# Attention followed by an FFN with x − tanh x: the clamps of the output weights' words go from VectorE to GpSimd, half of the first scalings to ScalarE, and the first batch is planned anew

## The chip, the cores and the metric

The kernel runs on one core of a Trainium2 chip. The time is in device microseconds, from the start to the end of one execution; the kernel before takes 1252.24 us (median of 3 runs, 1252.01 to 1252.95). Engines are named as in the profile: PE is TensorE's matmul, PEld its weight load, DVE is VectorE, ACT is ScalarE, POOL is GpSimd, SP issues DMAs.

## The reference

Keys and values are one tensor: `kv` pooled over windows of 4 by 4 and multiplied by `w_sr`. The output of the attention is the input of the FFN, whose activation is h − tanh h.

```python
B, C, H, W, N = 4, 128, 384, 32, 384 * 32
kv_pool = kv.reshape(B, H // 4, 4, W // 4, 4, C).mean(axis=(2, 4))
k = v = kv_pool.reshape(B, -1, C) @ w_sr           # 768 keys
s = (q @ k.transpose(0, 2, 1)) / np.sqrt(C)
a = np.exp(s - s.max(-1, keepdims=True))
x = (a / (a.sum(-1, keepdims=True) + 1e-9)) @ v    # 4 * 12288 tokens of 128
h = x @ w_in                                       # 128 -> 2048
return (h - np.tanh(h)) @ w_out                    # 2048 -> 128
```

`w_in` and `w_out` reach the kernel as 64-bit floats, so each weight is two 32-bit words that the kernel has to turn into one 32-bit float.

## The kernel before

The four batches are cut into 96 groups of 512 tokens, 24 to a batch. Tokens lie along the free axis, channels along the partitions. For each group `attention` makes scores in three pieces of 1024 columns (`scores`, PE, L1071), a root of them on ACT (`roots`, L1075, tile `p`), its square on POOL (`beyond`, L1078, tile `r2`, printed `r` in the profile), and the sum with the values on PE (`values`, L1121). Beside it goes a linear part: `upper_linear` (PE, L1093), `linear` (ACT, L1096, `yk`), `along` (POOL, L1099, `m`), `shares` (PE, L1102), `share_left` (ACT, L1105, `t`), `fewer` (DVE, L1111, `dy`), then `apart` (DVE, L1125, `dl`) and `rounded` (POOL, L1128, `dr`). The tiles of `y`, `den` and `num` share one bank of PSUM, `x`, one after the other. `feed_forward` multiplies `dr` by `winr` in eight pieces (`forth`, PE, L1178), squares them on ACT (L1182, `u`), makes cubes of them on DVE (L1185, `r`), and sums them with `Wr` and some smaller terms in one bank, `acc` (PE, L1197, L1164, L1168); `result` (DVE, L1208) takes it out.

Ahead of a batch's first group stands its preparation. For the first batch:

- `words_of` turns the words of a quarter of `w_in` or of `w_out` into floats: `size` (ACT, L438, the absolute value), `within` (DVE, L441, a clamp from above and below), `shift` (DVE, L444), `upper` (DVE, L448), `lower` (ACT, L454), `add` (DVE, L457). There are four quarters of each matrix. Every tile of 128x512 that `within` and `shift` use is one half of a tile of the ring `r` (for `w_out`).
- `keys` pools the keys (DVE, L588, and by halving sums on POOL, L582), takes their mean (`mean`, `centre`, L631) and multiplies by `w_sr` (L640, L652, L657).
- `about_centre` expands the FFN about the centre. `first` (PE, L764) gives the centre's h in the PSUM tile `prep` (bank `acc`). `first_chain`, 18 small DVE instructions on tiles of 128x16 (L850 to L876), gives slopes and their inverse, `third_order_apart` (seven more, L882 to L888) the third order. `by_first` (DVE, L953) scales a quarter of `winT` by g1, which lies in `prep`, into the tile `Wg`; `beside` (ACT, L961) puts a column of 4 from `prep` next to it; `slopes` (PE, L965) multiplies `Wg` by a quarter of `w_out` into `prep`. `spread` (PE, L936) and `scaled` (DVE, L943) scale `w_in` by the inverse into `winr`; `by_third` (POOL, L978) scales `w_out` by the third order into `Wr`. `turn_slopes`, `upper_slopes`, `joined_slopes`, `upper_joined` and `lower_joined` (L997 to L1011) end it.

Nothing runs in the order of the source. Each piece of work is handed to `Plan.op` with a step, an engine, an assumed duration (`us`), what it reads and writes, and its code. `Plan.run` starts what is ready in order of step, on assumed durations, and emits the code in the order in which it started it; each engine then runs its instructions in that order. `MOVES` is a table of numbers that are added to the steps. Where the planner treats two parts of one tile as apart, the waits between engines are still set by the framework for the emitted order. Names below carry the number of the buffer (`Wg_397`) where rows would read alike.

Of the kernel before, what the change touches and what calls it, by code (L numbers as in the profile page):

```python
# [207 lines left out]
def attention_then_ffn(ctx: ExitStack, tc: tile.TileContext, q, kv_by_key, kv_by_place, w_sr, w_in,  # L208
# [187 lines left out]
    def words_of(step, load_step, n, kind):  # L396
# [31 lines left out]
        def y(dt=F32):  # L428
            return plan[ym][:, 0].bitcast(dt)
# [1070 lines left out]
```

## Time and profile before

| | |
|---|---|
| median of 3 runs | 1252.24 us (1252.01 to 1252.95) |
| the profiled execution | 1249.61 us |
| its span, first to last instruction | 1247.9 us |
| PE busy | 1208.5 us (97%) |
| DVE busy | 1147.2 us (92%) |
| ACT busy | 1142.6 us (92%) |
| POOL busy | 1055.6 us (85%) |

The profile comes from one execution of 1249.61 us, of which 1.7 us lie outside the span. Times in its rows are counted from the start of the span. Busy time of PE is modelled from pipelined instructions, so the number of matmuls in a stretch says more than its share.

### The profile page before, as it was taken

Reading aid. Unit: us, or ns where it says so; the run is one execution under the profiler, and the core shown is the slowest. Engines: PE = TensorE matmul, PEld = TensorE weight load, DVE = VectorE, ACT = ScalarE, POOL = GpSimd, SP = SyncE. Lnnn points to the kernel's source line nnn. Section 1 sums busy time; section 2 is a strip of 40 time slices with the busy share of each in tenths; the row PEclk is TensorE's granted clock in tenths of the full one; section 3 lists DMA queues with packets and bytes.
Section 4 is the critical chain, followed back from the end, with each engine's and each line's share of the span. In section 5 each row is a group of like instructions: output and inputs, shape, how many; then the busy total and the mean of one; then the engine's idle time right before and its main releaser. Section 6 shows DMA issues by size and latency. Waiting matters only on the chain.

```text
span 1247.9 us, 16674 instructions
## 1 busy us (share of the span) xinstructions
PE 1208.5 (97%) x5252; PEld 929.5 (74%) x5252; DVE 1147.2 (92%) x1218; ACT 1142.6 (92%) x1373; POOL 1055.6 (85%) x836
## 2 busy tenths in 40 slices
PE   5899999999999999999999999999999999999997
PEld 4677777777777777777777777777777777777774
DVE  6789999989999999998999999999899999999997
ACT  3689998999999999999999998999999999999995
POOL 4599988799998887889999887789988888888881
PEclk8999999999999999999999999999999999999999
DMA  9134511125541111111563111111111111111101
GB/s 362 53 85 101 113 50 43 35 85 110 118 93 43 50 45 43 41 54 60 120 124 87 47 47 43 43 43 58 54 44 45 49 43 43 43 45 50 35 26 35
DMA packets 41713, 84.49 MB, mean 68 GB/s; under 512 B 5040, under 2 KB 7216, under 8 KB 41616
## 3 DMA queue, kind: packets, MB, share of 16 engines
q1 hardware_dynamic: 35904, 66.82, 16.1%
q0 software_dynamic: 5712, 16.52, 7.9%
q8 instruction: 44, 0.72, 0.2%
q14 instruction: 53, 0.43, 0.1%
HBM read 57.93 MB, written 25.39 MB: 67 GB/s over the span
## 4 chain that ended last, share of the span: by engine, by line
PE 80%; POOL 7%; DVE 5%; ACT 3%; issue 2%; DMA 2%; SPq 0%; DVEq 0%; ACTq 0%
PE big L1178 26%; PE acc L1197 24%; PE big L1071 9%; PE x L1121 9%; PE acc L1164 5%; POOL r L1078 3%; DVE r L1185 2%; PE x L1093 2%; PE x L1102 2%; PE acc L1168 1%; ACT u L1182 1%; ACT p L1075 1%; DMA winr<-in_kv_by_key_dram 1%; POOL dr L1128 1%; PE x L965 1%
## 5 line engine op out<-in xcount | busy, mean ns | idle before, releaser
L1185 DVE SCALAR_TENSOR_TENSOR r<-big,u 128x1024 fp32r<-128x1024 f32 x768 | 901.7, 1219 | 76.6 <-ACT u L1182 64.3
L1182 ACT ACTIVATE u<-big 128x1024 f32<-128x1024 f32 x768 | 762.4, 1028 | 42.1 <-PE big L1178 38.9
L1078 POOL TENSOR_TENSOR r<-p 128x1024 fp32r<-128x1024 f32 x288 | 562.9, 1961 | 107.9 <-ACT p L1075 107.5
L1178 PE MATMUL big<-dr,winr 128*128 128x512 f32 x1536 | 487.2, 407 | 5.0 <-ACT p L1075 2.7
L1197 PE MATMUL acc<-r,Wr 128*128 128x512 f32 x1536 | 451.3, 394 | 2.4 <-DVE o L1208 1.8
L1178 PEld LDWEIGHTS big<-dr,winr 128*128 128x128 f32 x1536 | 269.7, 188 | 107.9 <-DVE r L1185 29.7
L1197 PEld LDWEIGHTS acc<-r,Wr 128*128 128x128 f32 x1536 | 286.6, 188 | 68.9 <-DVE o L1208 2.6
L1075 ACT ACTIVATE p<-big 128x1024 f32<-128x1024 f32 x288 | 296.6, 1030 | 14.7 <-POOL r L1078 3.2
L1071 PE MATMUL big<-qr,kTr 128*128 128x512 f32 x576 | 185.7, 404 | 1.7 <-ACT p L1075 1.7
L1121 PE MATMUL x<-r,vvr 128*128 128x512 f32 x576 | 165.7, 396 | 1.2 <-POOL r L1078 0.8
L1128 POOL TENSOR_TENSOR dr<-dl,yk 128x512 fp32r<-128x512 f32 x96 | 130.4, 1358 | 40.4 <-DVE dl L1125 40.0
L1071 PEld LDWEIGHTS big<-qr,kTr 128*128 128x128 f32 x576 | 100.9, 188 | 40.9 <-ACT p L1075 22.5
L1115 POOL TENSOR_TENSOR ql<-q,qr 128x512 fp32r<-128x512 f32 x96 | 131.1, 1366 | 0.2
L1099 POOL TENSOR_TENSOR m<-yk,q 128x512 fp32r<-128x512 f32 x96 | 130.7, 1361 | 0.0
L1121 PEld LDWEIGHTS x<-r,vvr 128*128 128x128 f32 x576 | 108.5, 189 | 26.9 <-POOL r L1078 1.5
L1208 DVE TENSOR_SCALAR o<-acc,At 128x512 f32<-128x512 f32 x96 | 71.3, 743 | 1.5 <-PE acc L1168 1.5
L1111 DVE SCALAR_TENSOR_TENSOR dy<-x,yk 128x512 f32<-128x512 f32 x96 | 65.4, 681 | 1.6 <-ACT t L1105 1.6
L1056 POOL TENSOR_SCALAR qr<-q 128x512 fp32r<-128x512 f32 x96 | 65.8, 686 | 0.9 <-DMA q<-in_q_dram 0.7
L1125 DVE TENSOR_TENSOR dl<-x,dy 128x512 fp32r<-128x512 f32 x96 | 65.4, 681 | 0.3
L1096 ACT ACTIVATE yk<-x 128x512 f32<-128x512 f32 x96 | 57.9, 604 | 7.5 <-PE x L1093 6.4
L1164 PE MATMUL acc<-qr,Lh 128*128 128x512 f32 x192 | 60.4, 396 | 0.0
L1105 ACT ACTIVATE t<-x 128x512 f32<-128x512 f32 x96 | 57.8, 602 | 2.7 <-PE x L1102 2.3
(195 smaller groups left out, 629.7 us busy)
## 6 DMA issues: line engine op xcount, KB each, us to landing
q<-in_q_dram SPq DMA_DIRECT2D x96, 256.0 KB
out_dram<-o SPq DMA_DIRECT2D x96, 256.0 KB
kvp<-in_kv_by_place_dram POOLq DMA_DIRECT2D x21, 768.0 KB, 7.4
kc<-inverse SPq DMA_DIRECT2D x12, 256.0 KB
kvp<-in_kv_by_place_dram SPq DMA_DIRECT2D x3, 768.0 KB
winr<-in_kv_by_key_dram SPq DMA_DIRECT2D x4, 512.0 KB
r<-in_kv_by_key_dram SPq DMA_DIRECT2D x4, 512.0 KB
Wr<-in_kv_by_key_dram SPq DMA_DIRECT2D x4, 512.0 KB
```

What stands on the lines that cost most here:

```text
L1071: PE.matmul(out=half(plan[s], h), lhsT=plan[kTr][:, n * P : (n + 1) * P], rhs=plan[qr], start=True, stop=True)
L1075: A.activation(out=plan[p], in_=plan[s], func=AF.Silu, scale=1.0 / 3)
L1078: PL.tensor_tensor(out=plan[r], in0=plan[p], in1=plan[p], op=ALU.mult)
L1099: PL.tensor_tensor(out=plan[m], in0=plan[yk], in1=plan[qs], op=ALU.mult)
L1115: PL.tensor_tensor(out=plan[ql], in0=plan[qs], in1=plan[qr].bitcast(F32), op=ALU.subtract)
L1121: PE.matmul(out=plan[num], lhsT=plan[vvr][:, n], rhs=half(plan[f"r2.{g}.{k}"], h), start=(start and h == 0), stop=(stop and h == 1))
L1128: PL.tensor_tensor(out=plan[dr], in0=plan[dl].bitcast(F32), in1=plan[yk], op=ALU.add)
L1164: PE.matmul(out=plan[acc], lhsT=x, rhs=plan[y], start=(start and n == 0), stop=(stop and n == 2))
L1178: PE.matmul(out=half(plan[hp], h), lhsT=plan[winr][:, f * P : (f + 1) * P], rhs=plan[dr], start=True, stop=True)
L1182: A.activation(out=plan[u], in_=plan[hp], func=AF.Square)
L1185: V.scalar_tensor_tensor(out=plan[r], in0=plan[hp], scalar=1.0, in1=plan[u], op0=ALU.add, op1=ALU.mult)
L1197: PE.matmul(out=plan[acc], lhsT=plan[Wr][:, 2 * n + h], rhs=half(plan[r], h), start=(start and h == 0), stop=(stop and h == 1))
```

## The change

Four things are changed. `within` of `w_out`'s words runs on POOL, with an assumed duration of 0.66 us, and has a step of its own. `first_chain` gets one more DVE instruction, which copies g1 from `prep` to SBUF (`x(4)`). In the first batch the second and the fourth quarter (`n` odd) of `winT` are scaled by `pair_by_first` on ACT, two times two instructions of 128x128 for each, in place of one `by_first` on DVE. And the entries of `MOVES` for the first batch and for the first three groups are new; those of the other batches stand as they were.

```diff
     MOVES = {
-        "load.i.0": -4159.973, "words.i.0": -2510.035, "load.i.1": -4127.904, "words.i.1":
+        "load.i.0": -7340.706, "words.i.0": -3260.585, "load.i.1": -7340.702, "words.i.1":
...
         def within():
-            V.tensor_scalar(out=y(), in0=m(), scalar1=TOP, scalar2=BOTTOM, op0=ALU.min, op1=ALU.max)
+            E = V if kind == "i" else PL
+            E.tensor_scalar(out=y(), in0=m(), scalar1=TOP, scalar2=BOTTOM, op0=ALU.min, op1=ALU.max)
...
-        plan.op(step, "DVE", 0.36, within, (M,), (Y,), port=True)
+        plan.op(at(step, "within", kind, n), *(("DVE", 0.36) if kind == "i" else ("POOL", 0.66)), within, (M,), (Y,),
+                port=True)
...
             V.tensor_reduce(out=stat[:, b : b + 1], in_=z, op=ALU.add, axis=AX.X)
+            line(x(4), g1, 1.0, 0.0)
...
-            plan.op(known, on, 3.4, first_chain, ((prep, "h"),), ((prep, "t"), (hb, 8), iv, ("stat", b)))
+            plan.op(known, on, 3.55, first_chain, ((prep, "h"),), ((prep, "t"), (hb, 8), (hb, 4), iv, ("stat", b)))
...
-            if b:
+            if b or n % 2:
                 for k in range(2):
-                    plan.op(at(slopes_at[n], "pair", c, n, k), "ACT", 0.6, partial(pair_by_first, k), (gg, "winT"),
+                    plan.op(at(slopes_at[n], "pair", c, n, k), "ACT", 0.6, partial(pair_by_first, k),
+                            (gg if b else (hb, 4), "winT"),
                             ((wg, 2 + k),), late=0.1)
```

The lines of the kernel after are 3 to 7 higher than before (L1078 becomes L1085, L441 becomes L445).

On POOL, where the first batch's preparation gives way to the first groups (`q` to `qr` and `ql`, then the squares `r2`), there stood before:

```order
L1056 TENSOR_SCALAR qr_244<-q_193 128x512
L1056 TENSOR_SCALAR qr_251<-q_196 128x512
L1115 TENSOR_TENSOR ql_264<-q_196,qr_251 128x512
L1078 TENSOR_TENSOR r2_372<-p_340 128x1024
L1099 TENSOR_TENSOR m_383<-yk_351,q_141 128x512
```

and stands now:

```order
L1063 TENSOR_SCALAR qr_246<-q_193 128x512
L1063 TENSOR_SCALAR qr_253<-q_198 128x512
L1122 TENSOR_TENSOR ql_264<-q_198,qr_253 128x512
L445 TENSOR_SCALAR r_271<-r_271 128x512
L445 TENSOR_SCALAR r_279<-r_279 128x512
L445 TENSOR_SCALAR r_313<-r_313 128x512
L445 TENSOR_SCALAR r_320<-r_320 128x512
L1085 TENSOR_TENSOR r2_367<-p_333 128x1024
L1085 TENSOR_TENSOR r2_378<-p_372 128x1024
L1106 TENSOR_TENSOR m_400<-yk_376,q_123 128x512
```

The four clamps stand between the last `ql` and the first square, and `m` of the first group comes behind two squares where it came behind one.

On ACT, at the end of `first_chain` (`Wg` is the scaled quarter, `acc` the tile `prep`), with the semaphores that a row waits for, there stood before:

```order
L961 COPY Wg_392<-acc_259 128x4 [waits DVE_49]
L961 COPY Wg_397<-acc_259 128x4 [waits DVE_49]
L1105 ACTIVATE t_406<-x_399 128x512 [waits PE_49]
L961 COPY Wg_409<-acc_259 128x4 [waits DVE_49]
L1075 ACTIVATE p_425<-big_389 128x1024 [waits Pool_49]
```

and stands now:

```order
L967 COPY Wg_389<-acc_266 128x4 [waits DVE_49]
L964 ACTIVATE Wg_397<-winT_68,hb_347 128x128 x4
L967 COPY Wg_397<-acc_266 128x4 [waits DVE_49,PE_49]
L967 COPY Wg_418<-acc_266 128x4
L1082 ACTIVATE p_422<-big_386 128x1024 [waits Pool_49]
L1112 ACTIVATE t_431<-x_424 128x512 [waits PE_49]
```

The first group's `t` has moved behind a root (`p_422`), and the second column copy now waits for PE too.

On DVE, from the first group's `dy` to its `dl`, there stood before:

```order
L1111 SCALAR_TENSOR_TENSOR dy_431<-x_399,yk_351 128x512
L943 TENSOR_TENSOR winr_433<-big_401,win32_67 128x1024
L953 TENSOR_TENSOR Wg_409<-winT_68,acc_259 128x4x128
L953 TENSOR_TENSOR Wg_445<-winT_68,acc_259 128x4x128
L1125 TENSOR_TENSOR dl_457<-x_437,dy_431 128x512
```

and stands now:

```order
L1118 SCALAR_TENSOR_TENSOR dy_433<-x_424,yk_376 128x512
L949 TENSOR_TENSOR winr_441<-big_392,win32_67 128x1024
L949 TENSOR_TENSOR winr_441<-big_459,win32_67 128x1024
L452 SCALAR_TENSOR_TENSOR wout32_69<-Wr_203,r_320 128x512
L461 ISA wout32_69<-wout32_69,o_316 128x1024
L1132 TENSOR_TENSOR dl_481<-x_443,dy_433 128x512
```

The second half of `winr` and two steps of `w_out`'s words (the last quarter's `upper`, the third quarter's `add`) have come ahead of `dl`; the two scalings L953 between them are gone.

## Rows read from the trace of the kernel before

**Rows 1.** The page: the span.

```profile
span 1247.9 us, 16674 instructions
```

**Rows 2.** Busy time by stretch: start:end, length, PE and other engines with counts.

```profile
60.00:80.00 20.00, 18.79 (x75) 13.28 (x75) 14.52 (x15) 17.18 (x22) 18.64 (x14) 1.00 0.21 46
80.00:100.00 20.00, 19.25 (x78) 13.74 (x79) 17.45 (x17) 18.71 (x22) 19.26 (x15) 1.00 0.46 100
...
100.00:1200.00 1100.00, 1092.68 (x4699) 839.68 (x4698) 1031.81 (x1056) 1045.97 (x1249) 968.55 (x753) 1.00 0.23 61
```

**Rows 3.** Timeline of POOL: start, duration, instruction, count, idle time before and its releaser.

```profile
28.67 1.31 POOL L1056 TENSOR_SCALAR qr<-q 128x512 fp32r<-128x512 f32 x2 [0.71 <-DMA q<-in_q_dram]
30.07 1.33 POOL L1115 TENSOR_TENSOR ql<-q,qr 128x512 fp32r<-128x512 f32 x1
37.83 2.08 POOL L1078 TENSOR_TENSOR r<-p 128x1024 fp32r<-128x1024 f32 x1 [6.43 <-ACT p L1075]
...
51.25 1.27 POOL L1128 TENSOR_TENSOR dr<-dl,yk 128x512 fp32r<-128x512 f32 x1 [3.33 <-DVE dl L1125]
```

**Rows 4.** Timeline of ACT.

```profile
28.94 0.66 ACT L438 ACTIVATE r<-winr 128x512 f32<-128x512 f32 x1
...
42.39 0.60 ACT L1105 ACTIVATE t<-x 128x512 f32<-128x512 f32 x1
...
44.88 1.02 ACT L1075 ACTIVATE p<-big 128x1024 f32<-128x1024 f32 x1 [0.54 <-POOL r L1078]
```

**Rows 5.** Timeline of DVE, from the words of w_out to the first chain.

```profile
29.63 0.63 DVE L441 TENSOR_SCALAR r<-r 128x512 f32<-128x512 f32 x1 [1.27 <-ACT r L438]
30.30 1.39 DVE L444 TENSOR_SCALAR r<-r 128x512 int32<-128x512 int32 x1
...
37.02 0.42 DVE L444 TENSOR_SCALAR r<-r 128x512 int32<-128x512 int32 x1
...
38.08 0.17 DVE L853 TENSOR_SCALAR hb<-acc 128x16 f32<-128x16 f32 x1
```

**Rows 6.** Timeline of DVE, behind the first chain.

```profile
42.53 0.69 DVE L953 TENSOR_TENSOR Wg<-winT,acc 128x512 f32<-128x512 f32 x1 [0.23 <-ACT Wg L961]
...
47.76 1.23 DVE L943 TENSOR_TENSOR winr<-big,win 128x1024 fp32r<-128x1024 f32 x1 [2.26 <-PE big L936]
...
50.49 0.68 DVE L1125 TENSOR_TENSOR dl<-x,dy 128x512 fp32r<-128x512 f32 x1
...
54.51 1.56 DVE L457 CUSTOM_DVE_ANT_0 wout<-wout,o 128x1024 uint16<-128x1024 uint16 x1
```

**Rows 7.** Timeline of PE, from the first slopes to the first forth.

```profile
45.05 1.13 PE L965 MATMUL acc<-Wg,wout 128*128 128x129 f32 x8 [2.43 <-DVE hb L888]
...
47.38 2.67 PE L1121 MATMUL x<-r,vvr 128*128 128x512 f32 x6
...
51.59 0.47 PE L1102 MATMUL x<-m,share 128*128 128x512 f32 x1
...
53.91 1.56 PE L1178 MATMUL big<-dr,winr 128*128 128x512 f32 x6
```

**Rows 8.** PE by stretch of one microsecond: busy, granted clock, DMA.

```profile
45.00:46.00 1.00, 0.95 (x8) 1.00 0.00 0
46.00:47.00 1.00, 1.00 (x8) 0.62 0.00 0
...
48.00:49.00 1.00, 1.00 (x4) 0.50 0.00 0
```

**Rows 9.** Timeline of POOL, from the first wait behind the preparation on.

```profile
60.08 1.90 POOL L1078 TENSOR_TENSOR r<-p 128x1024 fp32r<-128x1024 f32 x1 [2.88 <-ACT p L1075]
...
65.53 1.90 POOL L1078 TENSOR_TENSOR r<-p 128x1024 fp32r<-128x1024 f32 x1 [1.28 <-ACT p L1075]
...
75.43 1.36 POOL L541 DMA_DIRECT2D kvp<-in_kv_by_place_dram  x1
...
93.06 1.29 POOL L1128 TENSOR_TENSOR dr<-dl,yk 128x512 fp32r<-128x512 f32 x1 [0.61 <-DVE dl L1125]
```

161 rows, old and new, of the table MOVES are left out of this document.

## The prediction

> **What bounds the kernel now.** I first read the busy time by stretch [rows 2]. From 100 to 1200 us PE is busy for 1092.68 of 1100 us with 4699 matmuls, 0.234 us each: in that part PE sets the time. From 60 to 80 us it does 75 matmuls and from 80 to 100 us 78, where 20 us at 0.234 would hold 85.4; some 18 are missing, 4.2 us of PE. Everything that this change touches lies ahead of 100 us. From about the 290th instruction on, the order on PE is the same before and after, so the change is worth what it shifts the point at which the common part begins. I take as that point the end of the fourth group's `dr` on POOL, 93.06 + 1.29 = 94.35 us [rows 9]; with it PE begins the fourth group's `forth`, and from there PE is nearly dense.
>
> Back from that point the chain is read engine by engine. POOL waits until 60.08 us for a root, once more 1.28 us at 65.53 and 0.61 us at 93.06 [rows 9], and hardly between. The root at 60.08 hangs on the first group's `forth` at 53.91 [rows 7], this on `dr` (51.25, after 3.33 us of waiting) and `dl` (50.49), `dl` on the first `values` (47.38), and these on the first `slopes` (45.05), which waited 2.43 us for the end of the third order on DVE [rows 3, 6, 7]. The third order follows `first_chain`, which begins at 38.08, when DVE is through with the words of `w_out`, begun at 29.63 [rows 5]. That is the path: words, first chain, slopes, values, `dl`, `forth`, root, POOL.
>
> **The clamps.** Four L441 leave DVE for POOL. On POOL the nearest row is the same kind of instruction on the same shape, two L1056 in 1.31 us, so 0.655 us each and 2.6 us for four; POOL idles 6.43 us ahead of 37.83 [rows 3], so they cost POOL nothing. But the order puts them behind the last `ql`, which ends at 30.07 + 1.33 = 31.40 [rows 3]; the first result is there at 32.05, where DVE had begun at 29.63. Ahead of it on PE, three more key products come before `centre` and delay the input from ACT (L438, 28.94 + 0.66 = 29.60 [rows 4]) by 3 x 0.234 = 0.7 us to 30.3; this is hidden behind `ql`, and would cost as much if `ql` were gone.
>
> From 29.63 to 38.08 DVE ran 15 instructions, 0.563 us each on average. The order leaves nine ahead of `first_chain`: besides the four clamps, one `upper` and one `add` have been put off. At the same average they take 5.1 us, so `first_chain` would start at 37.1. That is one bound. The other comes from L444 at 30.30: it took 1.39 us where the one at 37.02 took 0.42, and ended with POOL's `ql`, which was running [rows 3, 5]. DVE's steps here all stand beside clamps on POOL, and each may be held until a clamp ends; two such holds of 0.655 make it 38.4. I take the middle, 37.8: a gain of 0.3 where the removed instructions alone promise 1.0.
>
> The Trainium skill, "SBUF — State Buffer", section "Who interferes with whom", says that GpSimd and a VectorE instruction in its two-port mode, or with two SBUF inputs, exclude each other for a whole instruction, whichever starts first. The row of L444 agrees. By that rule alone every step of the words can be held, the first chain would start at the later bound, and the sum would come out 0.6 us above mine.
>
> **The first scalings.** From the start of `first_chain` to the first `slopes` it was 45.05 - 38.08 = 6.97 us [rows 5, 7]. One `by_first` that stood in between goes to ACT, 0.69 us and its wait of 0.23 [rows 6]; the copy of g1 adds about 0.2 (a small step takes 0.17 [rows 5]). So 6.25 us, and `slopes` starts at 37.8 + 6.2 = 44.0, 1.0 earlier.
>
> Here a new wait comes in. The second `beside` on ACT now also waits for PE: it reads `prep`, and the first `slopes` that writes `prep` has been emitted ahead of it. It can run only when that is done, 44.0 + 1.13 = 45.2 [rows 7]. Queued behind it on ACT are a root and then the first group's `t`. Before, `t` ran at 42.39, ahead of both [rows 4]. Now it ends at 45.2 + 1.02 + 0.60 = 46.8 [rows 4]. `dy` on DVE waits for `t` (0.69, priced like L953, of the same size [rows 6]) until 47.5, and the first group's `values` wait for `dy`, since `num` takes the bank of `den`. So `values` start at 47.5, against 47.38: the gain of 1.0 is used up. The four scalings on ACT themselves lie in this wait and cost nothing; without it they would hold ACT for two instructions' time each.
>
> **From `values` to `forth`.** Before, the six `values` stood together and `dl` came at 50.49 [rows 6]. Now four `values`, four `slopes` and eight `spread` come first: 16 x 0.234 = 3.7 us, to 51.2. DVE has to wait for these, because the second half of `winr` (1.23 [rows 6]) stands ahead of `dl` in its queue: 52.5. Then come the `upper` and the `add` that were put off, 2 x 0.563: 53.6. Then `dl`, 0.68: 54.3, where before it ended at 51.17. The third `slopes` and the third `by_third` wait for that `add` as well; on PE it ends at 53.6 + 1.13 = 54.7. From the second group's `shares`, next on PE, to `forth` it was 53.91 - 51.59 = 2.32 [rows 7]. So `forth` starts at 57.0, 3.1 us later. If an `add` beside POOL takes 1.56 like the one at 54.51 [rows 6], it is up to 0.9 more.
>
> **What comes back.** With `forth` 3.1 later, the root for which POOL waited until 60.08 comes at 63.2 too. From there to the fourth `dr` POOL ran 34.27 us, of which it waited 1.28 + 0.61 = 1.9 [rows 9]; with POOL later than the roots that it needs, these waits go. The squares, `dr`, `qr`, `ql` and `m` in that stretch are as many as before; one more DMA issue of the keys stands in it (1.36 [rows 9]), and `lower_joined` has gone out of it: I take 0.5 for both, from 0 to 1.4. The lag at the fourth `dr` is then 3.1 - 1.9 + 0.5 = 1.7 us, and PE carries it to the end.
>
> **Sum.** The profiled execution took 1249.61 us, 1247.9 of them the span [rows 1]. With 1.7 more it would take 1251.3. The median of the runs is 2.6 above the profiled one; I carry that over unchanged: 1252.24 + 1.7 = 1253.9 us. About 0.2%, 2.5 us, is what a measurement of this kernel can tell from no change; 1.7 lies inside.
>
> **Rivals.**
> (a) Slower: PE's clock falls while it waits. Before, it was granted 1.00 until 46 us, then 0.62 in one microsecond and 0.50, the lower level of 1.2 GHz, at 48 [rows 8], after PE had waited 2.43 us for `slopes`; the six `values` took 2.67 us, six `forth` 1.56 at the upper level [rows 7], 0.185 more each, and some ten products lay in it: 1.9 us. I have assumed that PE keeps 2.4 GHz through its new wait for `dy`, from 44.0 + 9 x 0.234 = 46.1 to 47.5. If it doesn't, the 16 products before the second half of `winr` pay the 1.9, all of it on the path: lag 3.6, 1255.8 us. Against it speaks that `slopes` start 1.0 earlier and PE's gaps are shorter; for it, that two gaps stand where one stood. It decides from 0.8 us on. Chance 0.31, with what else adds up to as much.
> The Trainium skill, "TensorE: Matmul & The Clock Gate", section "What's actually happening", says that the lower clock is the default and activity lifts it; the fall after the wait in these rows agrees.
> (b) Faster: the front isn't late. If `t` isn't held behind `slopes` and the root (1.13 + 1.02) and the first chain starts at 37.1 (0.7), `forth` starts at 57.0 - 2.9 = 54.1, the lag is -1.2 at the fourth `dr`, and if POOL's new order closes half of the 4.2 us of missing matmuls, -3.3: 1248.9 us. For it: DVE loses six long instructions ahead of `forth`; against it, the wait of the column copy that stands in the order. Chance 0.17.
> (c) The clamps relieve nothing: held at every step, the chain starts at 38.4, and all follows as above: 1254.5 us. That is inside the forecast's case, which with all that stays within 0.2% has 0.52.
>
> **Numbers.** Forecast 1253.9 us. The range goes down to 1250.0, a lag of -2.2, most of the way to (b), and up to 1256.5, (a) with 0.7 of the held `add`. Faster by over 0.2% 0.17, within 0.2% 0.52, slower by over 0.2% 0.31.
>
> **What would show it.** In the profile after, `first_chain` (L858) should begin near 37.8; a clamp on POOL should take 0.6 to 0.7 us; the second L967 should wait for PE until 45; L1112 should start near 46 and `values` (L1128) near 47.5; `dl` (L1132) near 53.6, `forth` (L1185) near 57.0; the fourth L1135 should end near 96. PE's granted clock should stay at 1.00 from 43 to 52. I am wrong if `t` comes ahead of the root's 1 us, if `dl` doesn't wait for the second half of `winr`, or if PE runs denser than before from 60 to 100 us.

## The result: 0.55% slower

The changed kernel takes 1258.09 us (median of 4 runs, 1257.37 to 1260.39) against 1252.12 for the kernel before (4 runs, 1251.23 to 1252.95): a ratio of 1.0055, with a 95% interval of 1.0043 to 1.0067, so 6.0 us by the medians (6.9 by the ratio, 5.4 to 8.4) where 1.7 were forecast, and above the range. The two profiled executions took 1257.83 and 1249.61 us and lie 8.2 apart. So places are read from the traces here, and sizes from the ratios.

The page and the busy time by stretch of the changed kernel, as in [rows 1, 2]:

```profile
span 1256.1 us, 16687 instructions
```

```profile
60.00:80.00 20.00, 17.15 (x72) 12.31 (x72) 13.86 (x14) 15.38 (x21) 13.96 (x11) 0.98 0.26 50
80.00:100.00 20.00, 19.54 (x80) 13.82 (x79) 16.58 (x17) 18.76 (x22) 19.27 (x14) 1.00 0.63 135
100.00:1200.00 1100.00, 1091.62 (x4691) 838.20 (x4690) 1030.51 (x1055) 1045.00 (x1247) 966.74 (x754) 1.00 0.22 60
```

Behind 100 us PE does 4691 matmuls where it did 4699, 8 fewer of 0.234 us, so little of the loss stands there. From 60 to 80 us POOL is busy for 13.96 us instead of 18.64: most of the loss stands ahead of 80 us.

The first weights landed 0.53 us later in this trace: ScalarE's first step on them started at 5.37 us instead of 4.84. Nothing is taken off the times below for it. e2, which has the same order, started at 4.88 and still reaches `first_chain` at 38.77, where the changed kernel has 38.72.

POOL, the timeline, as in [rows 3, 9]:

```profile
31.96 1.19 POOL L445 TENSOR_SCALAR r<-r 128x512 f32<-128x512 f32 x2
34.79 0.78 POOL L445 TENSOR_SCALAR r<-r 128x512 f32<-128x512 f32 x1 [1.64 <-ACT r L441]
...
55.66 1.26 POOL L1135 TENSOR_TENSOR dr<-dl,yk 128x512 fp32r<-128x512 f32 x1
...
65.71 3.75 POOL L1085 TENSOR_TENSOR r<-p 128x1024 fp32r<-128x1024 f32 x2 [0.47 <-ACT p L1082]
...
71.49 1.88 POOL L1085 TENSOR_TENSOR r<-p 128x1024 fp32r<-128x1024 f32 x1 [0.69 <-ACT p L1082]
...
99.05 1.31 POOL L1135 TENSOR_TENSOR dr<-dl,yk 128x512 fp32r<-128x512 f32 x1
```

DVE, the timeline, as in [rows 5, 6]:

```profile
32.61 0.82 DVE L448 TENSOR_SCALAR r<-r 128x512 int32<-128x512 int32 x1 [2.94 <-POOL r L445]
...
35.01 1.10 DVE L452 SCALAR_TENSOR_TENSOR wout<-winr,r 128x512 int32<-128x512 int32 x1
...
38.72 0.17 DVE L858 TENSOR_SCALAR hb<-acc 128x16 f32<-128x16 f32 x1
...
52.15 1.23 DVE L949 TENSOR_TENSOR winr<-big,win 128x1024 fp32r<-128x1024 f32 x1 [2.84 <-PE big L942]
53.30 0.68 DVE L452 SCALAR_TENSOR_TENSOR wout<-Wr,r 128x512 int32<-128x512 int32 x1
53.89 0.69 DVE L461 CUSTOM_DVE_ANT_0 wout<-wout,o 128x1024 uint16<-128x1024 uint16 x1
54.50 0.69 DVE L1132 TENSOR_TENSOR dl<-x,dy 128x512 fp32r<-128x512 f32 x1
...
77.79 0.74 DVE L1215 TENSOR_SCALAR o<-acc,At 128x512 f32<-128x512 f32 x1
```

ACT, the timeline, as in [rows 4]:

```profile
45.81 0.23 ACT L967 COPY Wg<-acc 128x4 f32<-128x4 f32 x2 [2.35 <-PE acc L971]
45.92 1.04 ACT L1082 ACTIVATE p<-big 128x1024 f32<-128x1024 f32 x1
46.84 0.62 ACT L1112 ACTIVATE t<-x 128x512 f32<-128x512 f32 x1
...
64.62 1.02 ACT L1082 ACTIVATE p<-big 128x1024 f32<-128x1024 f32 x1
```

PE, the timeline, as in [rows 7], and PE's granted clock (the figure behind the bracket) by the microsecond, as in [rows 8]:

```profile
44.65 1.13 PE L971 MATMUL acc<-Wg,wout 128*128 128x129 f32 x8 [1.38 <-DVE hb L894]
...
48.24 1.20 PE L1128 MATMUL x<-r,vvr 128*128 128x512 f32 x4 [1.33 <-DVE dy L1118]
...
54.64 1.16 PE L971 MATMUL acc<-Wg,wout 128*128 128x129 f32 x8 [2.05 <-DVE wout L461]
...
57.49 0.79 PE L1100 MATMUL x<-qr,Mh 128*128 128x512 f32 x1 [1.46 <-DVE dy L1118]
58.08 1.05 PE L1185 MATMUL big<-dr,winr 128*128 128x512 f32 x2
58.94 1.88 PE L971 MATMUL acc<-Wg,wout 128*128 128x129 f32 x8
```

```profile
57.00:58.00 1.00, 0.51 (x1) 0.61 0.02 10
58.00:59.00 1.00, 1.00 (x4) 0.50 0.07 16
59.00:60.00 1.00, 1.00 (x6) 0.50 0.00 0
60.00:61.00 1.00, 1.00 (x6) 0.68 0.00 0
```

The forecast wait is there: the column copy L967 waits 2.35 us for PE's `slopes`, a root stands behind it, then `t`. What was not forecast stands further on. Behind two waits of PE, 2.05 us for the words and 1.46 us for the second group's `dy`, the clock falls to its lower level, 1.2 GHz, and the fourth `slopes` take 1.88 us instead of 1.13. The root for which POOL waits comes at 64.62, 5.6 us later than before, and the first result (L1215) 6.0 later, though the first `forth` is only 4.2 later. The same two places in the kernel before:

```profile
58.98 1.02 ACT L1075 ACTIVATE p<-big 128x1024 f32<-128x1024 f32 x1
```

```profile
71.78 0.74 DVE L1208 TENSOR_SCALAR o<-acc,At 128x512 f32<-128x512 f32 x1
```

### The profile page after: what moved, and what is told of

Same layout as the page of the kernel before. It is cut to its first block, busy times and chain, and to the rows that moved or that the text cites. A ratio compares the mean times of both kernels' runs of the same rounds, so it can differ in the third digit from the quotient of the medians.

```text
span 1256.1 us, 16687 instructions
## 1 busy us (share of the span) xinstructions
PE 1210.9 (96%) x5252; PEld 930.7 (74%) x5252; DVE 1143.7 (91%) x1213; ACT 1145.1 (91%) x1381; POOL 1057.3 (84%) x840
## 4 chain that ended last, share of the span: by engine, by line
PE 85%; DVE 5%; ACT 4%; issue 2%; DMA 2%; POOL 1%; SPq 0%; ACTq 0%; DVEq 0%; POOLq 0%
PE big L1185 27%; PE acc L1204 25%; PE big L1078 10%; PE x L1128 9%; PE acc L1171 5%; DVE r L1192 3%; ACT u L1189 2%; PE x L1100 2%; PE x L1109 2%; PE acc L1175 2%; ACT p L1082 1%; PE x L971 1%; DMA Wr<-in_kv_by_key_dram 1%; DMA q<-in_q_dram 1%; DMA winr<-in_kv_by_key_dram 1%
## 5 line engine op out<-in xcount | busy, mean ns | idle before, releaser
L1085 POOL TENSOR_TENSOR r<-p 128x1024 fp32r<-128x1024 f32 x288 | 561.5, 1956 | 103.6 <-ACT p L1082 103.3
L1078 PE MATMUL big<-qr,kTr 128*128 128x512 f32 x576 | 185.8, 404 | 1.5 <-ACT p L1082 1.4
L1078 PEld LDWEIGHTS big<-qr,kTr 128*128 128x128 f32 x576 | 100.8, 188 | 40.2 <-ACT p L1082 20.5
L1215 DVE TENSOR_SCALAR o<-acc,At 128x512 f32<-128x512 f32 x96 | 71.3, 742 | 2.5 <-PE acc L1175 1.5
```

Of the source, the lines that this page charges most:

```text
L1078: PE.matmul(out=half(plan[s], h), lhsT=plan[kTr][:, n * P : (n + 1) * P], rhs=plan[qr], start=True, stop=True)
L1085: PL.tensor_tensor(out=plan[r], in0=plan[p], in1=plan[p], op=ALU.mult)
```

## The experiments

In the variants that move single steps, the list of steps is sorted as in the changed kernel, and then one step is put ahead of another; `("add", 6), ("scaled", 1)` means that step 6 of the name `add`, counted from 0, is emitted just ahead of step 1 of the name `scaled`. The table holds what all eighteen came to. "First result" is where DVE starts the first group's output (L1208 before, L1215 after). Its last column is the median ratio to the kernel before, run beside it on the same chip.

| kernel | first `forth` | root on ACT | first result | ratio, 95% interval |
|---|---|---|---|---|
| before | 53.91 | 58.98 | 71.78 | 1 |
| after | 58.08 | 64.62 | 77.79 | 1.0055, 1.0043 to 1.0067 |
| e1 | 57.09 | 62.00 | 74.99 | 1.0010, 1.0001 to 1.0019 |
| e2 | 57.87 | 63.18 | 76.37 | 1.0040, 1.0027 to 1.0054 |
| e3 | 53.69 | 58.09 | 72.63 | 0.9995, 0.9986 to 1.0004 |
| e4 | 55.10 | 59.06 | 71.45 | 0.9993, 0.9984 to 1.0002 |
| e5 | 57.25 | 64.60 | 78.57 | 1.0055, 1.0041 to 1.0068 |
| e6 | 56.92 | 63.46 | 76.63 | 1.0042, 1.0028 to 1.0055 |
| e7 | 58.17 | 64.54 | 77.70 | 1.0062, 1.0048 to 1.0076 |
| e8 | 52.37 | 61.25 | 74.41 | 1.0028, 1.0017 to 1.0038 |
| e9 | 57.60 | 64.16 | 78.78 | 1.0047, 1.0033 to 1.0061 |
| e10 | 58.49 | 63.99 | 80.41 | 1.0059, 1.0046 to 1.0073 |
| e11 | 54.15 | 58.97 | 71.93 | 0.9986, 0.9977 to 0.9995 |
| e12 | 51.91 | 59.54 | 73.86 | 1.0018, 1.0009 to 1.0027 |
| e13 | 52.66 | 60.05 | 74.05 | 1.0008, 0.9998 to 1.0017 |
| e14 | 55.38 | 59.34 | 71.71 | 0.9981, 0.9972 to 0.9990 |
| e15 | 56.98 | 62.30 | 76.58 | 1.0027, 1.0017 to 1.0037 |
| e16 | 58.10 | 61.99 | 76.83 | 1.0037, 1.0023 to 1.0052 |
| e17 | 56.70 | 61.52 | 75.24 | 1.0013, 1.0004 to 1.0022 |
| e18 | 56.14 | 60.12 | 74.17 | 0.9993, 0.9984 to 1.0002 |

**e1: does a delay at the first `forth` come back?** In the kernel before:

```diff
-            PL.tensor_tensor(out=plan[dr], in0=plan[dl].bitcast(F32), in1=plan[yk], op=ALU.add)
+            for _ in range(1 if g else 3):
+                PL.tensor_tensor(out=plan[dr], in0=plan[dl].bitcast(F32), in1=plan[yk], op=ALU.add)
```

> The kernel before, with the first group's dr on POOL written three times instead of once (twice the same again, the values unchanged): two more additions of 1.27 us, so the first forth starts 2.5 us later and nothing else is touched. Theory 1 (my forecast's term): POOL's later waits for roots, 1.9 us, swallow most of a delay at the first forth, so the time grows by about 0.6 us, to 1252.7. Theory 2 (carry): the roots that POOL waits for hang on the same chain and come later with it, so the waits stay and the time grows by the whole 2.5 us, to about 1254.6, or by 3 to 4 us if PE's granted clock falls in the longer wait.

POOL's timeline in e1, and PE's where `forth` begins:

```profile
53.06 3.97 POOL L1129 TENSOR_TENSOR dr<-dl,yk 128x512 fp32r<-128x512 f32 x3 [4.21 <-DVE dl L1125]
...
63.10 1.89 POOL L1078 TENSOR_TENSOR r<-p 128x1024 fp32r<-128x1024 f32 x1 [1.62 <-ACT p L1075]
...
68.73 1.89 POOL L1078 TENSOR_TENSOR r<-p 128x1024 fp32r<-128x1024 f32 x1 [1.47 <-ACT p L1075]
...
96.25 1.29 POOL L1129 TENSOR_TENSOR dr<-dl,yk 128x512 fp32r<-128x512 f32 x1 [0.63 <-DVE dl L1125]
```

```profile
57.09 1.67 PE L1179 MATMUL big<-dr,winr 128*128 128x512 f32 x6 [1.25 <-POOL dr L1129]
```

POOL's later waits, 1.28 and 0.61 us before [rows 9], are 1.47 and 0.63 here. The first `forth` is 3.18 us later than before, the fourth `dr` 3.19 and the last result 3.22. Nothing comes back: theory 2. Of the 3.18, 1.8 stand ahead of the edit: `dr` begins at 53.06 instead of 51.25, since `first_chain` came 0.9 later in this execution and PE's clock fell earlier, under the first `slopes` (2.06 us instead of 1.13). The two additions, 2.5 us, moved `forth` by only 1.4, because before it had started 1.4 us behind the end of `dr` (52.52). The measured time grew by 1.3 us (0.1 to 2.4). That fits 1.4 us carried in full, but it holds theory 1's 0.6 as well and does not decide; the trace does.

**e2: what the fallen clock costs.** In the changed kernel, ahead of the third `slopes` and of the third `upper_linear`, into a spare tile:

```diff
+            PE.matmul(out=spare[:, (k % 8) * P : (k % 8 + 1) * P], lhsT=ident, rhs=ident, start=True, stop=True)
```

> The changed kernel, with products of the identity that nobody reads put into PE's two waits ahead of the first forth: 14 records (1.8 us) ahead of the third slopes, where PE idles 2.05 us for the words of w_out, and 8 records (1.05 us) ahead of the third group's upper_linear, where it idles 1.46 us for dy. Theory K (clock): the granted clock stays at 1.00 from 57 to 61 us, where it was 0.61, 0.50, 0.50 and 0.68, and the 1.5 us that the lower level took there come back: about 1256.6 against 1258.1. Rival: the engines behind PE set the time there, the clock is held up all the same and the time stays within 0.5 us of the changed kernel's.

DVE's start of `first_chain`, PE's clock, its timeline, and ACT's, in e2:

```profile
38.77 0.17 DVE L858 TENSOR_SCALAR hb<-acc 128x16 f32<-128x16 f32 x1
```

```profile
58.00:59.00 1.00, 1.00 (x10) 1.00 0.00 0
```

```profile
58.32 1.05 PE L975 MATMUL acc<-Wg,wout 128*128 128x129 f32 x8
```

```profile
63.18 1.02 ACT L1086 ACTIVATE p<-big 128x1024 f32<-128x1024 f32 x1
```

From `first_chain` to 57.5 us the trace is that of the changed kernel within 0.05 us. Behind it the clock stays up, the fourth `slopes` take 1.05 us, and the root comes 1.44 us earlier; so does the first result (1.42). Theory K holds by the trace. The ratios differ by 0.0015, 1.9 us, but their intervals overlap.

**e3, e4, e17, e18: which part of the change.** e3 has the changed kernel's steps and the table of before. e4 has the table of the change and the old steps; e17 puts only the scalings back to DVE (and leaves out the copy of g1, which they no longer need), e18 only the clamps:

```diff
e4, e18
-            E = V if kind == "i" else PL
-            E.tensor_scalar(
+            V.tensor_scalar(
e4, e17
-            if b or n % 2:
+            if b:
```

> The changed kernel's instructions (clamps of w_out on GpSimd, half of the first scalings on ScalarE, the copy of g1) with the table of before. Theory O (order): the loss lies in the new table's order between 44 and 58 us, so with the old table the first forth starts within 1 us of 53.9 and the time is 1251.5 to 1253.5. Rival (instructions): the clamps on GpSimd and the wait of beside cost it whatever the order, and the time stays at 1256 or above.

> The kernel before's instructions (all clamps and all first scalings on VectorE) under the new table. Theory O (order): the new table alone makes it slow, so 1256 or above, with the first forth at 57 us or later. Rival (instructions): without the clamps on GpSimd and the scalings on ScalarE the front is as before and the time is within 1.5 us of 1252.1.

> The new table with the clamps of w_out on GpSimd, but all first scalings on VectorE as before. Theory I (only both steps together, under this table, push the first group's last values behind the spread and the first three forth apart): the three forth stand together ahead of the third slopes, the first result comes within 1 us of 71.8, and the ratio to the kernel before lies between 0.998 and 1.002. Rival C (the clamps on GpSimd do it): 1.004 or more.

> The new table with half of the first scalings on ScalarE, but the clamps on VectorE as before. Theory I: the first result comes within 1.5 us of 71.8, and the ratio lies between 0.998 and 1.002. Rival P (the scalings on ScalarE do it, since beside and the root wait behind slopes there too): 1.004 or more.

Theory O held for e3 and fell for e4: the new table alone is not slow, and neither are the new steps alone. With one changed step under the new table it is 1.6 us (clamps, 0.5 to 2.8) and nothing (scalings); with both 6.9 by the ratio. In e4, e17 and e18 the first three `forth` stand ahead of the fourth quarter's `slopes`, with at most one other product between them; only with both changes does the list come out with two word steps ahead of `dl` and the `forth` split. The last `values` stand behind the `spread` in e17 as well. The ratios bear theory I out; the profiled executions of e17 and e18 put the first result 3.5 and 2.4 us later than before, further than it allowed, with PE's clock at its lower level for nearly 7 us in each (43 to 47 and 56 to 61 us in e17, 44 to 52 in e18).

**e5, e6, e7: the three latenesses that the forecast named.** The changed kernel with:

```diff
e5
+("beside", 1), ("pair_by_first", 0)   ("beside", 2), ("pair_by_first", 0)   ("shares", 0), ("slopes", 0)
e6
+("upper", 7), ("scaled", 1)   ("add", 6), ("scaled", 1)
e7
+("values", 2), ("slopes", 1)   ("apart", 0), ("scaled", 1)   ("rounded", 0), ("by_third", 2)
```

> The changed kernel with three steps emitted earlier and nothing else: the second and the third beside on ScalarE ahead of the four scalings, and the first shares on PE ahead of the first slopes, so that neither the beside nor the root and the first group's t behind it wait for slopes. Theory B (the new wait that I forecast): the root starts near 43.7 instead of 45.9 us, t near 44.7, the first values near 46.0 instead of 48.2, the first forth 2 us earlier (near 56), and since nothing behind it catches up, the time falls by 2 us, to about 1256, or to 1254.5 if the clock holds as well. Rival W (the words set it): the first forth stays within 0.5 us of 58 and the time within 0.7 us of 1258.1.

> The changed kernel with the put-off upper and add of w_out's third quarter on DVE ahead of the second half of winr instead of behind it, into the 2.84 us in which DVE waits for PE's spread. Theory W (the words set it): the third slopes start at about 52.7 instead of 54.6 us without the wait of 2.05 us, the first forth near 56.6 instead of 58.1, and the time falls by 1.5 us, or by 2.9 us if PE's clock holds at 1.00 from 57 to 61: 1255.2 to 1256.6. Rival (dl sets it): dl comes only 0.5 to 1.2 us earlier, and the time falls by no more than that.

> The changed kernel with the first group's last two values on PE ahead of the second slopes, dl on DVE ahead of the second half of winr, and dr on POOL ahead of the third by_third. Theory D (my forecast's reading that dl's lateness sets the first forth): dl ends near 51 instead of 55.2 us and the time falls by 2 us or more. Rival W: the first forth stands on PE behind the third slopes, the second group's shares and the third group's upper_linear, which wait for the words' add, for t and for dy; dl was no longer the one that came last, the add comes 0.4 us later, and the time stays or grows by 0.4 us: 1258.1 to 1258.6.

e5 brought `values` and the first `forth` forward by only 0.8 us, since the next scaling on DVE reads the tile `prep` as well and waited 1.32 us for the `slopes` in its turn; the clock then stood at 0.50 from 56 to 62 us, and the root came where it was. e6 was worth 1.6 us by the ratio, with intervals that overlap, and 1.2 in its trace (`forth` and the first result), with the clock still falling: the words did stand in the way. e7 refutes theory D: `dr` ended 4.8 us earlier, and the first `forth` came at 58.17 all the same. (The `upper` of e6 is that of the last quarter, the `add` that of the third.)

**e8, e12: the front rebuilt.** e8 has the moves of e5 to e7 and two `forth` with their `dr`, square and cube ahead of the third `slopes`; e12 goes further:

```diff
e8, beside e5 to e7
+("rounded", 0), ("slopes", 2)   ("forth", 0), ("slopes", 2)   ("forth", 1), ("slopes", 2)
+("square", 1), ("share_left", 1)   ("cube", 0), ("fewer", 1)
e12, beside e8
+("add", 7), ("scaled", 1)   ("slopes", 3), ("shares", 1)   ("forth", 2), ("upper_linear", 2)
+("square", 4), ("share_left", 1)   ("cube", 1), ("fewer", 1)   ("sum_slopes", 0), ("upper_linear", 2)
+("turn_slopes", 0), ("upper_linear", 2)   ("upper_slopes", 0), ("linear", 2)   ("roots", 5), ("upper_joined", 0)
```

> The changed kernel with the moves of the three runs beside it together, and the first two forth on PE ahead of the third slopes (with their dr, the first square on ScalarE and the first cube on VectorE moved up to match). If the lateness of the first forth is what costs the 6 us and it carries one to one, the first forth starts near 52 us or earlier (58.1 in the changed kernel, 53.9 before), and the time falls by 5 to 7 us, to 1251 to 1253, which is the kernel before or a little under it. Rival (the changed instructions themselves cost time behind the front): it stays above 1255 though forth is early.

> The changed kernel with all moves of e8, and further: the last add of w_out's words on DVE and the fourth slopes on PE ahead of the second group's shares, the third forth, the turning of the slopes and its copies behind them, two squares on ScalarE ahead of t, and the root ahead of upper_joined. First forth near 52.4 as in e8 (58.1 in the changed kernel), the fourth slopes near 54.5 (60.8 and 56.1 before), the root near 59.3 (64.6 and 59.0 before). If the lateness of both, first forth and root, is all that the new table costs, the time is within 1 us of the kernel before, 1251 to 1253. If the changed instructions cost time further back, it stays above 1254.

PE and ACT, the timelines, in e8:

```profile
52.37 1.18 PE L1195 MATMUL big<-dr,winr 128*128 128x512 f32 x4
```

```profile
61.25 1.02 ACT L1092 ACTIVATE p<-big 128x1024 f32<-128x1024 f32 x1
```

Both missed: a first `forth` 1.5 to 2 us earlier than before still leaves them 0.28% and 0.18% slower than before. The medians, 1255.17 and 1254.24, lie just above the bounds of the rival, that the changed instructions cost time further back (1255 and 1254). Against it stands e3, which has these instructions under the old table and is not slower (0.9995); it is not refuted for the new table. In e8 the fourth `slopes` come at 56.73, and on ACT two squares and five small copies stand between them and the root.

**e9, e10, e16: the root or the squares.** Single moves on ACT in the changed kernel; e16 is e2 with the root first on ACT and its square first on POOL:

```diff
e9
+("square", 4), ("square", 2)
e10
+("roots", 5), ("square", 4)
e16, beside e2
+("roots", 5), ("square", 4)   ("beyond", 4), ("lower_joined", 0)
```

> The changed kernel with one step of ScalarE moved: the square of the second forth ahead of the square of the third, the order in which PE makes them and in which the cubes of DVE want them (as it stands, DVE waits 1.73 us for the later one). Theory S (the chain forth, square, cube, next forth sets the time behind the first forth): the two cubes begin near 62.8 instead of 64.25 us, the next forth near 64.2 instead of 65.6, and the time falls by 1.4 us, to about 1256.7. Theory R (the first root behind the preparation, on ScalarE at 64.62, sets it): the root stays where it is or comes up to 0.6 us earlier, and so does the time: 1257.5 to 1258.1.

> The changed kernel with that root on ScalarE moved ahead of the third square and of the two copies of upper_joined, nothing else. Theory R: the root starts near 63.2 instead of 64.6 us, POOL's square near 64.3 instead of 65.7, and the time falls by 1.4 us, to about 1256.7. Theory S: the third square comes 1 us later, and with it the cube and the next forth, and the time grows by 1 us, to about 1259.

> The kernel of e2 (clock held up) with the first root on ScalarE ahead of the third square and of upper_joined, and the square of it on POOL ahead of lower_joined, which in e10 stood in its way. Theory R (the root that POOL waits for sets the time): POOL's square starts near 63 instead of 64.3 us and the ratio falls from 1.0040 to about 1.0029. Theory S (the chain forth, square, cube sets it): the third square and its cube come 1 us later and the ratio grows to about 1.0048.

ACT and DVE, the timelines, in e16:

```profile
61.99 1.02 ACT L1096 ACTIVATE p<-big 128x1024 f32<-128x1024 f32 x1
```

```profile
63.96 3.49 DVE L1215 SCALAR_TENSOR_TENSOR r<-big,u 128x1024 fp32r<-128x1024 f32 x3 [2.64 <-ACT u L1212]
```

e10 does not test theory R: POOL's square stood behind `lower_joined`, which waits for ACT, and started at 66.91, later than before the move. e16 does: root and POOL's square come 1.2 us earlier than in e2, the second cube 1.15 later, and the first result 0.46 later (0.23 of it already at the first `forth`). By the trace R falls. The ratio, 1.0037, has an interval that holds what R wanted (1.0029) and what S wanted (1.0048), so S is left open in size. In e9 the cubes came at 62.09 and still the first result 1 us later in the profile, since a new wait of 1.25 us for POOL's square let PE's clock fall again. PE and its clock in e9:

```profile
67.20 1.19 PE L1138 MATMUL x<-r,vvr 128*128 128x512 f32 x2 [1.25 <-POOL r L1095]
```

```profile
68.00:69.00 1.00, 1.00 (x3) 0.50 0.00 0
```

**e11, e13, e14, e15: the clock held up elsewhere.** e11 is the kernel before and e14 is e4, with the first `spread` made three times; e13 is e12 with the third `forth` repeated three times in PE's waits; e15 is e6 with the products of e2 (2 and 5 instructions):

```diff
e11, e14
-                        for n in range(FW):
+                        for n in list(range(FW)) * (3 if j == k == 0 else 1):
e13, once ahead of turn_slopes, once ahead of and once behind the third upper_linear
+            again[0, 4]()
```

> The kernel before with its first spread on PE written three times instead of once (the same products into the same places, 2.1 us more), which fills the 2.43 us in which PE idles ahead of the first slopes. PE's granted clock then stays at 1.00 from 46 to 50 us, where it was 0.62, 0.50, 0.50 and 0.68. Theory S: spread, values and dl come 1.0 to 1.2 us earlier, the first forth near 52.8 instead of 53.9, and the time falls by 1 us, to about 1251 (median of before 1252.1). Theory R: the third quarter's add (54.5), the fourth slopes behind it (56.1) and the root (59.0) stay, and the time stays within 0.4 us.

> The kernel of e12 with the third forth on PE written three times more (the same products into the same place, 0.46 us each), in the waits of 0.74, 0.24 and 0.69 us between 55.6 and 58.2, after which the granted clock stood at 0.50 from 59 to 62 us. Theory K (the clock eats what the earlier front gains): the clock stays at 1.00, the products of 59 to 62 take 1.7 us less, and the time falls from 1.0018 of the kernel before to about 1.0005. Rival: the earlier front is worth no more than e12 showed, for the engines behind PE, and the ratio stays at 1.0014 to 1.0022.

> The kernel of e4 (all steps as before, under the new table) with its first spread written three times, as in e11, which fills the 2.07 us of PE ahead of the first slopes, where the granted clock fell to 0.50 from 46 to 48 us. Theory K: the clock stays at 1.00 and 1 to 1.5 us come back, so 0.9982 to 0.9987 of the kernel before, below both kernels. Rival: the words of w_out set the front there, and the ratio stays at 0.9993.

> The kernel of e6 (the put-off upper and add ahead of the second half of winr) with products nobody reads in PE's waits ahead of the third slopes' shares (4 records) and of the third upper_linear (10 records), so that the clock, 0.50 from 56 to 59 us in e6, stays at 1.00. Theory K: e6 gained 1.2 us and e2 1.7; they are two causes and add up, so the ratio falls from 1.0042 to about 1.0030. Rival: both take away the same lateness, and the ratio stays at 1.0038 to 1.0042.

PE's clock in e12 and in e13:

```profile
60.00:61.00 1.00, 1.00 (x5) 0.50 0.00 0
```

```profile
60.00:61.00 1.00, 1.00 (x6) 1.00 0.00 0
```

In e11 the clock stays at 1.00 in the whole front (30 to 76 us) and the kernel before becomes 0.14% faster (0.05 to 0.23). Where that comes from its trace doesn't show: `first_chain` came 0.9 us later in this execution, the first `forth` 0.2 later (54.15), and the root at the same time (58.97). By the ratio e13 gains 0.10% on e12, and words and clock add up in e15 (1.0027; 1.0042 with the words alone, 1.0040 with the clock alone), but these intervals overlap, and the traces show no gain: the first result comes at 74.05 in e13 (73.86 in e12) and at 76.58 in e15 (76.37 in e2). In both the clock was held up where it should be and fell elsewhere, at 45 to 48 us in e13, at 44 to 47 and 64 to 67 in e15. e14 is 0.19% below the kernel before and so below both kernels. But in its profiled execution the clock fell at 43 us, behind a wait of 1.55 us ahead of the repeated products, and stayed low to 46 us under them; that it gains over e4 (0.9993) is not clear of the noise, and the cause is not shown.

## Why the prediction was wrong

**Right, place by place, to about 1 us.** The first clamp's result was there at 32.56 us (forecast 32.05); `first_chain` began at 38.72 (37.8, bounds 37.1 and 38.4); `slopes` at 44.65 (44.0); `t` ended at 47.46 (46.8); `values` began at 48.24 (47.5), `dl` at 54.50 (53.6), the first `forth` at 58.08 (57.0). The clamps took 0.60 to 0.86 us each. The new wait of `beside` came where it was forecast, and ate the gain as forecast. Two steps beside clamps were held: L448 took 0.82 us instead of 0.42, L452 1.10 instead of 0.68, 0.8 us in all. This is the exclusion that the Trainium skill, "SBUF — State Buffer", "Who interferes with whom", states; the 38.4 worked out for it was nearer to the 38.72 than my 37.8. (L444 before, from which I read the hold, ended at 31.69, 0.3 us behind `ql` and not with it.)

One trace can't tell a place closer than that. Twelve traces have the changed kernel's order up to `first_chain` and begin it at 38.07 to 39.37. The kernel before begins it at 38.08, but e1 and e11, which are the same up to there, at 39.02 and 39.01. So the gain of 0.3 us that I forecast for the clamps isn't to be seen.

```profile
39.02 0.17 DVE L853 TENSOR_SCALAR hb<-acc 128x16 f32<-128x16 f32 x1
```

**The step that failed: "What comes back".** I let POOL's waits of 1.9 us swallow the delay, and so came from 3.1 to 1.7. e1 shows that the roots which POOL waits for come later by as much as POOL does, so that the waits stay: the term is 0 where I had -1.4. The changed kernel shows the same: from the square of that root to the end of the fourth `dr` POOL took 34.65 us (65.71 to 100.36), where it had been 34.27 and I had 34.27 - 1.9 + 0.5 = 32.9. The forecast treated the wait as POOL's own slack, while the root hangs on the same chain of PE, ACT and DVE.

**The second: PE's clock.** I assumed that it would keep 2.4 GHz, and looked for a fall in one wait only, at 46 to 47.5 us. There it held. It fell one stage on, behind the waits for the words' `add` and for the second group's `dy`; in e5, e6, e7, e9 and e10, which also add no products there, it falls between 55 and 59 us too. e2 gives the price, from one trace: 1.4 us. Rival (a) had the mechanism and nearly the price (1.9), at the wrong place.

**Sizes.** Between the two traces the first `forth` is 4.2 us later, not 3.1. From there to the first result the clock's 1.4 come in, and 0.4 more whose cause no run shows. From the first to the fourth result 41.72 us pass instead of 41.06; all kernels whose order behind the first result comes from the new table have these 0.7 (41.70 to 41.76), those with the old table have 41.02 to 41.09. I had put both at nothing, since I took all that changes to lie ahead of 100 us; PE's order is the same from there on, but POOL's only from 157 us. So 4.2 + 1.4 + 0.4 + 0.7 = 6.7 up to the fourth result; 0.4 more between it and the 95th and 1.0 in the last group (below) make 8.1 of the 8.2 by which the profiled executions differ. The medians differ by 6.0. The rest belongs to the single executions: the kernel before was traced in one that took 2.5 us less than its median, and it reached `first_chain` 0.9 us ahead of e1 and e11. Each of these sizes is good to about 1 us, and their sum proves nothing closer.

**The anchor.** The point to which I carried the lag, the fourth `dr`, is 6.0 us later (100.36 against 94.35), as the first result is: the point was good, the path to it was not. I measured the change at the first `forth`, through a root that I tied to it. e8 moves the first `forth` 5.7 us forward and the first result only 3.4. In all twenty traces the time from the first result to the 95th is the same within 1.7 us, while the first result itself lies between 71.45 and 80.41. That is the point to which such a front is to be costed.

**Open.** Which chain holds e8 and e12 between `forth` and the first result was not settled: the root alone does not (e16), and for the squares its interval is too wide to tell. With the fall at 59 us held up (e13) 0.08% are left, with an interval that reaches to no difference. Why the list of steps comes out badly only with both changes was not followed through the planner.

## What to carry to other kernels

A wait of another engine on the same chain is not slack: before letting it absorb a delay, follow what it waits for, and see whether that is late by as much. Cost a changed start at the first output from which on all variants run alike. And look at every wait of PE that a new order leaves, not only at the one that the change puts in: in e5, e9 and e12 a gain at the front was partly eaten by a clock that fell in the next gap.

## What the runs showed of the hardware

The granted clock does not follow from the order of the instructions and the length of a wait alone. e13 has e12's instructions up to 55 us, and in both PE waits 0.71 us ahead of the first `slopes`. In e12 the clock stays at 1.00 there; in e13 it falls to 0.50, and the `slopes` take 1.75 us instead of 1.13. PE's timeline in e12 and in e13:

```profile
44.53 1.13 PE L981 MATMUL acc<-Wg,wout 128*128 128x129 f32 x8 [0.71 <-DVE hb L904]
```

```profile
45.09 1.75 PE L981 MATMUL acc<-Wg,wout 128*128 128x129 f32 x8 [0.71 <-DVE hb L904]
```

It is the same with e16, whose clock falls at 43 to 47 us where that of e2 does not. Only e2, e3 and e11 show no fall from 30 to 76 us. So a kernel in which one fall is held up can have another in its place, and a price taken from two traces holds for these two.

In the last group PE waits 1.78 to 1.80 us for the same output in all twenty traces. In fifteen of them the clock stays at 1.00, and the last result follows the one before it after 8.24 to 8.26 us; in five (the changed kernel, e2, e6, e7, e8) it falls to 0.50 and that takes 9.27 to 9.52. PE's timeline there, in the kernel before and in the changed one:

```profile
1234.01 0.73 PE L1197 MATMUL acc<-r,Wr 128*128 128x512 f32 x2 [1.79 <-DVE o L1208]
1234.58 1.30 PE L1178 MATMUL big<-dr,winr 128*128 128x512 f32 x4
```

```profile
1241.12 0.80 PE L1204 MATMUL acc<-r,Wr 128*128 128x512 f32 x2 [1.78 <-DVE o L1215]
1241.72 1.91 PE L1185 MATMUL big<-dr,winr 128*128 128x512 f32 x4
```

The Trainium skill, "TensorE: Matmul & The Clock Gate", "What's actually happening", has the lower clock as the default that activity lifts. e2 and e11, which only add products and show no fall in the front, agree; in e13, e15 and e16 products were added too, and the clock fell elsewhere. Why the same wait ends differently, no run here tells.
